# A fused linear-attention and mixture-of-experts kernel: the attention's scans read their second operand from PSUM, and the first tiles are issued in another order

## Chip, cores and metric

The kernel runs on one core of one Trainium2 chip. The metric is the device time of one execution in microseconds (us). Five engines work side by side, each through its own queue in order: PE (TensorE, matmuls), DVE (VectorE), ACT (ScalarE), POOL (GpSimd) and SP (SyncE, which here issues nearly all DMAs). They wait for one another through semaphores.

## The reference, cut to what matters

```
# gated linear attention, batch 4, 8 heads, 768 steps, head size 48
for t in range(768):
    state = alpha[t][:, None] * state + outer(k[t], v[t])
    y[t] = q[t] @ state
# y becomes x [3072, 384]; then a mixture of 8 experts, one expert per token:
xn, en = x / |x|, expert_emb / |expert_emb|
logits = xn @ en.T / tau
e = argmax(logits);  gate = softmax(logits)[e]
x2 = gate * (relu(x @ w1[e]) @ w2[e])
# then a dense layer pair with an ELU between
h = x2 @ w_in;  out = where(h > 0, h, exp(h) - 1) @ w_out
```

Everything is float32.

## The kernel before, in words

The program has three stages: attention with routing (the first 172 us of the profiled execution), the experts (to about 440 us) and the dense pair (to the end). The change touches only the first.

**Attention.** The 768 steps are cut into six chunks of 128, and with four batches there are 24 tiles, numbered 0 to 23, chunk by chunk. A tile holds eight heads as four pairs in the free dimension (`NP`), with 112 partitions for the two heads of a pair. For every tile the decays `alpha` are turned into running products. DVE does this with two scans over the 517 columns of the tile's `at` (four segments of 129 and one more column):

- `stR` (L332): the scan `R` (L340) runs backwards with multiply and then max against the tile `back`; it gives the product from a step to the chunk's end. A small reciprocal (L341) of each segment's first value goes into the tile `fore`. POOL then multiplies the keys: `Kh = k * R` (L343).
- `stA` (L345): the scan `A` (L350) runs forwards with multiply and then add of `fore`, so each segment starts from that reciprocal. POOL multiplies the queries: `Qh = q * A` (L352).

The two second operands, `back` and `fore`, are tiles of 112x517 in SBUF, as are `at`, `R` and `A`.

The other steps of a tile: `stE` (L354) copies checkpoints of `A` on ACT. `stS` (L371) makes the scores `psS` on PE from `Kh` and `Qh`; `stP` (L382) multiplies them by the triangle on DVE, from PSUM, in two halves `P`. `stT` (L360) transposes `Kh` on PE, and ACT copies it to `Kt` (L367). `stC` (L391) makes `psY` on PE from `P` and `v` (and from the state `G` in all but the first chunk), ACT copies it to `yT` (L407), and PE makes the state's update `psU`. `stD` (L439) makes `psX` on PE from `yT` and `rhsX`, which holds the normed expert embeddings beside an identity: `psX` has the token rows and, added up by a DVE reduce (L451), the logits. `psX` has two PSUM buffers.

**The order of the turns.** A hand-written loop (`fast`, L636) takes one turn per tile. Turn i issues, in this order: the loads of tile i+4 (for `v`, i+3), `stS` and `stT` of tile i+1, then `stR` of tile i+2, the first half of `stP` of tile i+1, `stA` of tile i+2, the second half of `stP`, the scatter of finished rows on POOL (`put`, L550), the reduces of the logits, pending routing work (`stR1`, `stR2`, small DVE operations on groups of two to six tiles), then `stD` of tile i-1, `stE` of tile i+2 and `stC` of tile i. Each engine follows this order within its own queue. So a tile's `Qh` is made one turn ahead of its `psS`.

**Before the loop** (L637 to L678): the first loads; 11 matmuls without use (`warm`, L281, L651) that keep PE active; `stR` and `stA` of tiles 0 and 1; the square sum of the embeddings on ACT (L668); `stS`, `stT` and `stP` of tile 0; casts of three constants on DVE. The embeddings' norm is a Newton iteration (`inv_norm1`, L127) in small DVE operations that stand in the queue `todo` and run in turns 0 and 1; the scaling of the embeddings (L675) and their transposition (`eT`, L725) close turn 1, and `stD` of tiles 0 and 1 both follow in turn 2.

Of the kernel before, what the change touches and what calls it, by code (L numbers as in the profile page):

```python
# [8 lines left out]
F32 = mybir.dt.float32  # L9
# [17 lines left out]
TP = T + 1  # L27
SW = H // 2 * TP + 1
# [20 lines left out]
A_FLOOR = 1e-15  # L49
# [12 lines left out]
def fused_kernel(ctx, tc, qk, a, v, emb, w12, wi, wo, cst, sel, cols, out):  # L62
# [64 lines left out]
    def inv_norm1(pool, x):  # L127

        shape = [x.shape[0], 1]
        y = pool.tile(shape, F32, name="rs_y1")  # L130
        t = pool.tile(shape, F32, name="rs_t1")
        h = pool.tile(shape, F32, name="rs_h1")
        yi = y.bitcast(I32)
        steps = [
            lambda: nc.vector.tensor_scalar(yi, x.bitcast(I32), 1, None, op0=ALU.logical_shift_right),
            lambda: nc.vector.tensor_scalar(h, x, -0.5, None, op0=ALU.mult),
            lambda: nc.vector.tensor_scalar(yi, yi, -1.0, float(0x5F3759DF), op0=ALU.mult, op1=ALU.add),
        ]
# [148 lines left out]
    def attention():  # L287
        with ExitStack() as st:
# [15 lines left out]
            back = gp.tile([C2, SW], F32, name="back")  # L304
            fore = [gp.tile([C2, SW], F32, name=f"fore{i}") for i in range(2)]
# [4 lines left out]

            def seg(t, n=TP):

                return t[:, :NP * TP].rearrange("c (p t) -> c p t", t=TP)

# [17 lines left out]
            def stR(i):  # L332

                if i >= NT:
                    return
                R = Rs[i] = wk.tile([C2, SW], F32, name="R")
                nc.vector.tensor_tensor_scan(R[:, ::-1], at[i][:, ::-1], back[:, ::-1], 0.0, op0=ALU.mult, op1=ALU.max)  # L340
                nc.vector.reciprocal(seg(fore[i % 2])[:, :, 0:1], seg(R)[:, :, 1:2])  # L341
                Kh[i] = wk.tile([C2, NP, T], F32, name="Kh")
                nc.gpsimd.tensor_tensor(Kh[i], qkt[i][:, 1], R[:, 1:].rearrange("c (p t) -> c p t", t=TP)[:, :, 1:], op=ALU.mult)  # L343

            def stA(i):  # L345

                if i >= NT:
                    return
                A = As[i] = wk.tile([C2, SW], F32, name="A")
                nc.vector.tensor_tensor_scan(A, at.pop(i), fore[i % 2], 0.0, op0=ALU.mult, op1=ALU.add)  # L350
                Qh[i] = wk.tile([C2, NP, T], F32, bufs=3, name="Qh")
                nc.gpsimd.tensor_tensor(Qh[i], qkt.pop(i)[:, 0], seg(A)[:, :, 1:], op=ALU.mult)  # L352

            def stE(i):  # L354
                if i < NT:
                    nc.scalar.activation(out=chk[:, i], in_=seg(As.pop(i))[:, :, 0:TP:T], func=AF.Copy)
# [68 lines left out]
            def stH(i):  # L425

                if i >= NT:
                    return
                r = Rs.pop(i)
                if i >= B:  # L430
                    g = G[i % B]
                    for p in range(NP):
                        nc.scalar.activation(out=g[:, p, :D], in_=g[:, p, :D], func=AF.Copy, scale=seg(r)[:, p, 1:2])
# [5 lines left out]
            def stD(i, keep=False):  # L439
# [4 lines left out]
                x = psD.tile([128, NP, 128], F32, name="psX")  # L444
# [73 lines left out]

            def stR2(g):
# [3 lines left out]
                r = ps1.tile([128, 8, E], F32, tag="psT" if g == NG - 2 else "psR", name="psR")[:, :n]  # L523
# [50 lines left out]
            def general():  # L574
# [15 lines left out]
                with tc.For_i(0, NC, 1) as cc, tc.For_i(0, T // TB, 1) as tb:  # L590
                    ts = bass.ds(tb * TB, TB)
                    for b in range(B):
                        for p in range(NP):
                            for h2 in range(2):
                                p0 = (b * H + 2 * p + h2) * EG
                                ch = slice(h2 * HP, h2 * HP + D)
                                for nm, src in (("a", a[bass.ds(cc, 1), ch, b, bass.ds(tb * TB + (p * TP + 1), TB)]),
                                                ("k", qk[bass.ds(cc, 1), ch, b, 1, p, ts]),
                                                ("q", qk[bass.ds(cc, 1), ch, b, 0, p, ts])):
                                    nc.sync.dma_start(out=rows[nm][p0:p0 + EG], in_=src.to_broadcast([EG, D, TB]))  # L600
# [35 lines left out]
            def fast():  # L636
# [14 lines left out]
                warm(ps1, "psY", 11)  # L651
                nc.scalar.activation(out=warm_t, in_=ones, func=AF.Exp)
                nc.vector.memset(back, A_FLOOR)
                nc.vector.memset(back[:, 1:].rearrange("c (p t) -> c p t", t=TP)[:, :, T:], 1.0)
                nc.vector.memset(cum[:, 0], 0.0)
                for t in fore + G:
                    nc.gpsimd.memset(t, 0.0)
                zero = xp.tile([128, 1, XW], F32, tag="xt", name="zero")
                nc.gpsimd.memset(zero, 0.0)
                for j in range(2):  # L660
                    stR(j)
                    stA(j)
                    stE(j)
                    stH(j)
                rows, rtau = emb_t[:, :2 * NP * HP], emb_t[:, 2 * NP * HP:]
                es = sm.tile([E, 1], F32, name="es")
                esq = wk.tile([E, 2 * NP * HP], BF16, bufs=1, tag="junk", name="esq")
                nc.scalar.activation(out=esq, in_=rows, func=AF.Square, accum_out=es)  # L668
                en, steps = inv_norm1(sm, es)
                stS(0)  # L670
                stT(0)
                stP(0, 0)
                stP(0, 1)
                todo.extend([lambda: nc.vector.reciprocal(rtau, rtau)] + steps
                            + [lambda: nc.vector.tensor_scalar(rows, rows, en, rtau, op0=ALU.mult, op1=ALU.mult)])  # L675
                nc.vector.tensor_tensor(strict16, c["tri"], c["ident"], op=ALU.subtract)
                nc.vector.tensor_copy(ident16, c["ident"])
                nc.vector.tensor_copy(base16[:, 0], c["base"])  # L678
# [3 lines left out]
                for i in range(tail):  # L682
# [9 lines left out]
                    if i - 3 in last:  # L692
                        todo[:0] = stR2(last[i - 3])
                    stR(i + 2)
                    stP(i + 1, 0)
                    stA(i + 2)
# [18 lines left out]
                    if i == 2:  # L715
                        stD(0)
                    if i > 1:
# [3 lines left out]
                    if i == 1:  # L721
                        step(len(todo))
                        eT = ps1.tile([128, NP, E], F32, tag="psR", name="eT")
                        for p in range(NP):
                            nc.tensor.transpose(eT[:, p], rows[:, p * 128:(p + 1) * 128], c["ident"][:E, :E])  # L725
                        nc.vector.tensor_copy(rhsX[:, :, CW:CW + E], eT)
# [21 lines left out]
            def decays():  # L748
# [3 lines left out]
                t = ps1.tile([1, 1], F32, tag="psR", name="psB")  # L752
# [14 lines left out]
            def ending():  # L767
# [9 lines left out]
                stP(i + 1, 1)  # L777
                r = stR2(g2 - 1)
# [446 lines left out]
def _layout(inputs):  # L1225
# [70 lines left out]
```

## Time and profile before

| what | us |
|---|---|
| three runs | 806.57, 808.1, 811.5 (median 808.1) |
| the profiled execution's own time | 807.42 |
| its span, from its first to its last instruction | 805.6 |
| attention with routing, up to the first expert matmul | 172.0 |
| mean granted TensorE clock, share of full speed | 0.988 |

The profile records one execution. Its span lies 1.8 us below its own time, and that time 0.7 us below the median of the runs. Times in rows are counted from the span's start. In a timeline row the columns are: start in us, length in us, engine, line, operation, output<-inputs, partitions x elements, and in brackets the engine's idle time before it and what ended that. A row with a count (x16) takes neighbouring instructions together.

### The profile page before, as it was taken

Reading aid. Unit: us, or ns where it says so; the run is one execution under the profiler, and the core shown is the slowest. Engines: PE = TensorE matmul, PEld = TensorE weight load, DVE = VectorE, ACT = ScalarE, POOL = GpSimd, SP = SyncE. Lnnn points to the kernel's source line nnn. Section 1 sums busy time; section 2 is a strip of 40 time slices with the busy share of each in tenths; the row PEclk is TensorE's granted clock in tenths of the full one; section 3 lists DMA queues with packets and bytes.
Section 4 is the critical chain, followed back from the end, with each engine's and each line's share of the span. In section 5 each row is a group of like instructions: output and inputs, shape, how many; then the busy total and the mean of one; then the engine's idle time right before and its main releaser. Section 6 shows DMA issues by size and latency. Waiting matters only on the chain.

```text
span 805.6 us, 13707 instructions
## 1 busy us (share of the span) xinstructions
PE 774.2 (96%) x5064; PEld 700.7 (87%) x5064; DVE 538.6 (67%) x1015; ACT 358.0 (44%) x783; POOL 190.1 (24%) x218
## 2 busy tenths in 40 slices
PE   7799998889999999999999999999999999999996
PEld 5688877669999999999988899999999999999996
DVE  7779999956877788888467665454545545545442
ACT  2466877624554555555355443333333333323331
POOL 6433656612333343343000020010002002002002
PEclk7899999999999999999999999999999999999999
DMA  9988863266656557563000010000001001000001
GB/s 246 255 237 216 229 182 95 109 196 157 194 184 206 179 193 231 173 213 111 1 0 1 2 40 1 0 11 31 1 1 39 1 1 40 0 1 30 11 1 39
DMA packets 44805, 77.72 MB, mean 96 GB/s; under 512 B 11958, under 2 KB 18230, under 8 KB 44734
## 3 DMA queue, kind: packets, MB, share of 16 engines
q1 hardware_dynamic: 41662, 67.36, 28.9%
q0 software_dynamic: 3072, 9.45, 3.2%
q8 instruction: 40, 0.66, 0.4%
q14 instruction: 31, 0.25, 0.1%
HBM read 64.58 MB, written 12.22 MB: 95 GB/s over the span
## 4 chain that ended last, share of the span: by engine, by line
PE 39%; issue 30%; DVE 3%; POOL 2%; ACT 2%; POOLq 0%; ACTq 0%
PE h L1144 6%; PE y L988 5%; PE y L990 4%; PE y L989 4%; PE h L957 4%; PE h L958 4%; PE h L956 4%; POOL out_dram L1178 2%; PE o L1167 2%; PE o L1165 2%; PE o L1166 2%; PE t L937 1%; DVE dlo L260 1%; DVE g L1150 1%; DVE mn L1146 1%
## 5 line engine op out<-in xcount | busy, mean ns | idle before, releaser
L1146 DVE TENSOR_SCALAR mn<-h 128x512 f32<-128x512 f32 x96 | 66.2, 690 | 139.7 <-PE h L1144 139.7
L1147 ACT ACTIVATE mn<-mn 128x512 f32<-128x512 f32 x96 | 60.7, 633 | 171.9 <-DVE mn L1146 171.9
L1167 PE MATMUL o<-dwo,gl 128*128 128x384 f32 x384 | 129.4, 337 | 1.4 <-DVE gl L1154 1.4
L1166 PE MATMUL o<-dlo,gh 128*128 128x384 f32 x384 | 128.4, 334 | 0.0
L1165 PE MATMUL o<-dwo,gh 128*128 128x384 f32 x384 | 128.2, 334 | 0.0
L1144 PE MATMUL h<-xh,dwi 128*128 128x512 f32 x288 | 112.8, 391 | 0.6 <-ACT x2T L1002 0.6
L1144 PE MATMUL h<-xh,dlo 128*128 128x512 f32 x288 | 113.2, 393 | 0.0
L1144 PE MATMUL h<-xl,dwi 128*128 128x512 f32 x288 | 112.5, 392 | 0.0
L1178 POOL DMA_INDIRECT out_dram<-ob,ids x24 | 23.2, 966 | 341.8 <-ACT ob L1175 338.1
L1153 ACT ACTIVATE gh<-g 128x512 fp32r<-128x512 f32 x96 | 60.7, 633 | 77.6 <-DVE g L1150 77.6
L960 ACT ACTIVATE hh<-h 128x432 fp32r<-128x432 f32 (+6 forms) x64 | 32.4, 507 | 106.2 <-PE h L958 99.1
L204 DVE TENSOR_TENSOR wlo<-raw,whi 128x512 fp32r<-128x512 f32 x96 | 73.2, 789 | 5.6 <-ACT whi L201 4.8
L1150 DVE SCALAR_TENSOR_TENSOR g<-mn,h 128x512 f32<-128x512 f32 x96 | 66.1, 688 | 15.2 <-ACT mn L1147 14.7
L1165 PEld LDWEIGHTS o<-dwo,gh 128*128 128x128 f32 x384 | 72.0, 187 | 4.2
L1166 PEld LDWEIGHTS o<-dlo,gh 128*128 128x128 f32 x384 | 72.0, 187 | 4.0
L1167 PEld LDWEIGHTS o<-dwo,gl 128*128 128x128 f32 x384 | 72.2, 188 | 2.1 <-DVE gl L1154 1.7
L961 DVE SCALAR_TENSOR_TENSOR hl<-h,hh 128x432 fp32r<-128x432 f32 (+6 forms) x64 | 36.7, 573 | 47.6 <-ACT hh L960 46.2
L988 PE MATMUL y<-hh,whi 128*128 128x432 f32 (+6 forms) x192 | 68.4, 356 | 0.0
L956 PE MATMUL h<-xh,whi 128*128 128x432 f32 (+6 forms) x192 | 66.5, 346 | 0.7 <-ACTq L1015 0.7
L244 POOL TENSOR_SCALAR dg<-dg 128x384 f32<-128x384 f32 x32 | 42.0, 1312 | 106.3 <-ACT dg L243 106.2
L1154 DVE TENSOR_TENSOR gl<-g,gh 128x512 fp32r<-128x512 f32 x96 | 65.7, 684 | 1.2 <-ACT gh L1153 1.1
L958 PE MATMUL h<-xh,wlo 128*128 128x432 f32 (+6 forms) x192 | 66.4, 346 | 0.0
(210 smaller groups left out, 1520.5 us busy)
## 6 DMA issues: line engine op xcount, KB each, us to landing
raw<-in_w_dram SPq DMA_DIRECT2D x96, 256.0 KB, 3.3
qk<-in_qk_dram SPq DMA_DIRECT2D x40, 192.0 KB, 3.9
vt<-in_v_dram SPq DMA_DIRECT2D x24, 256.0 KB, 4.7
raw<-in_wi_dram SPq DMA_DIRECT2D x16, 384.0 KB, 4.3
raw<-in_wo_dram SPq DMA_DIRECT2D x16, 384.0 KB, 4.1
xr<-xs SPq DMA_DIRECT2D x7, 576.0 KB, 4.9
at<-in_alpha_dram SPq DMA_DIRECT2D x40, 96.9 KB, 3.0
xs<-zero SPq DMA_DIRECT2D x7, 288.8 KB, 5.5
```

What stands on the lines that cost most here:

```text
L204: nc.vector.tensor_tensor(l[:, sl], r, h[:, sl].bitcast(F32), op=ALU.subtract)
L956: nc.tensor.matmul(ps, wh, xh[:, kk], start=(kk == 0), stop=False)
L958: nc.tensor.matmul(ps, wl, xh[:, kk], start=False, stop=(kk == KD - 1))
L988: nc.tensor.matmul(acc[e][d], wh, hh, start=(f == 0), stop=False)
L1144: nc.tensor.matmul(ps, l, x, start=(n == 0), stop=(n == len(terms) - 1))
L1146: nc.vector.tensor_scalar(mn, ps, 0.0, None, op0=ALU.min)
L1147: nc.scalar.activation(out=mn, in_=mn, func=AF.Exp)
L1150: nc.vector.scalar_tensor_tensor(g, mn, -1.0, ps, op0=ALU.add, op1=ALU.max)
L1154: low.append(lambda: nc.vector.tensor_tensor(gl, g, gh.bitcast(F32), op=ALU.subtract))
L1165: nc.tensor.matmul(o_, gh[:, sl], wh, start=(f == 0), stop=False)
L1166: nc.tensor.matmul(o_, gh[:, sl], wl, start=False, stop=False)
L1167: nc.tensor.matmul(o_, gl[:, sl], wh, start=False, stop=(f == M - 1))
```

## The change

The scans take their second operand from PSUM. A new tile `pz` takes one PSUM bank; one column of it, set to 2^-50, is broadcast over the tile's width as `floor`. For that, `at` gets three more columns per segment (`LEAD`): a zero, a 1/floor and a place for the reciprocal, and a 1/floor at its end, so that a segment now has 132 columns and a tile 528. The scan `R` takes the max with `floor`; the scan `A` takes the max with it too, starts afresh at every segment through the zero and the 1/floor, and finds the reciprocal in `at` itself. The tiles `back` and `fore` are gone, with their memsets on DVE and POOL.

In the first tiles: the embeddings are loaded ahead of tile 1 instead of behind it; 20 matmuls without use stand at the start instead of 11, and 4 more behind `stT` of tile 0; the Newton iteration runs on ACT ahead of the loop (only its first guess stays on DVE), its last reciprocal and the scaling in turn 0, `eT` at the end of turn 0; `stD` of tile 0 comes in turn 1 and so on, one per turn. The casts of the constants go to turn 3, on ACT and POOL.

Since the bank of `psR` is now that of `pz`, the routing's count tile takes a buffer of `psX` in most groups (`count_tile`), and the pending reduces are issued ahead of it.

```diff
+LEAD = 3
+TP = LEAD + T + 1
+SW = NP * TP
+A_FLOOR = 2.0 ** -50
...
-        yi = y.bitcast(I32)
...
+        yi, vec, act = y.bitcast(I32), nc.vector, nc.scalar
+        first = [
+            lambda: vec.tensor_scalar(yi, x.bitcast(I32), 1, None, op0=ALU.logical_shift_right),
+            lambda: vec.tensor_scalar(yi, yi, -1.0, float(0x5F3759DF), op0=ALU.mult, op1=ALU.add),
+        ]
+        steps = [lambda: act.activation(out=h, in_=x, func=AF.Copy, scale=-0.5)]
         for _ in range(3):
             steps += [
+                lambda: act.activation(out=t, in_=y, func=AF.Copy, scale=h),
+                lambda: act.activation(out=t, in_=t, func=AF.Copy, scale=y),
+                lambda: act.activation(out=t, in_=t, func=AF.Copy, bias=1.5),
+                lambda: act.activation(out=y, in_=t, func=AF.Copy, scale=y),
             ]
+        steps += [lambda: act.activation(out=y, in_=y, func=AF.Copy, scale=x, bias=1e-6)]
...
-            back = gp.tile([C2, SW], F32, name="back")
-            fore = [gp.tile([C2, SW], F32, name=f"fore{i}") for i in range(2)]
+            pz = pz_p.tile([128, 512], F32, name="pz")
+            floor = pz[:C2, 0:1].to_broadcast([C2, SW])
...
-                nc.vector.tensor_tensor_scan(R[:, ::-1], at[i][:, ::-1], back[:, ::-1], 0.0, op0=ALU.mult, op1=ALU.max)
-                nc.vector.reciprocal(seg(fore[i % 2])[:, :, 0:1], seg(R)[:, :, 1:2])
+                nc.vector.tensor_tensor_scan(R[:, ::-1], at[i][:, ::-1], floor, A_FLOOR, op0=ALU.mult, op1=ALU.max)
+                nc.vector.reciprocal(seg(at[i])[:, :, LEAD - 1:LEAD], seg(R)[:, :, LEAD:LEAD + 1])
...
-                nc.vector.tensor_tensor_scan(A, at.pop(i), fore[i % 2], 0.0, op0=ALU.mult, op1=ALU.add)
+                nc.vector.tensor_tensor_scan(A, at.pop(i), floor, 0.0, op0=ALU.mult, op1=ALU.max)
...
+            def count_tile(g):
+
+                if pz is None:
+                    return ps1.tile([128, 8, E], F32, tag="psR", name="psR")
+                if g == NG - 1:
+                    return pz[:, 64:64 + 8 * E].rearrange("p (n e) -> p n e", e=E)
+                if g == NG - 2:
+                    return ps1.tile([128, 8, E], F32, tag="psT", name="psR")
+                return psD.tile([128, 8, E], F32, tag="psX", name="psR")
...
                 nc.sync.dma_start(out=cs, in_=cst)
+                nc.sync.dma_start(out=emb_t, in_=emb)
                 load(1)
                 load_v(0)
-                nc.sync.dma_start(out=emb_t, in_=emb)
...
-                warm(ps1, "psY", 11)
+                warm(ps1, "psY", 20)
...
                 stS(0)
                 stT(0)
+                warm(ps1, "psY", 4)
+                for f in guess:
+                    f()
+                nc.vector.reciprocal(rtau, rtau)
+                stE(1)
                 stP(0, 0)
                 stP(0, 1)
+                for f in newton:
+                    f()
...
                     stP(i + 1, 0)
+                    if i == 0:
+                        nc.vector.reciprocal(en, en)
+                        nc.scalar.activation(out=rows, in_=rows, func=AF.Copy, scale=en)
+                        nc.scalar.activation(out=rows, in_=rows, func=AF.Copy, scale=rtau)
                     stA(i + 2)
...
-                    if i == 2:
-                        stD(0)
-                    if i > 1:
+                    if i > 0:
                         stD(i - 1)
```

On DVE the instructions from the scan `A` of tile 1 to the scan `A` of tile 2 stand so before (`strict`, `ident` and `base` are the casts; the numbers behind `at` and `fore` are those of buffers):

```order
L350 SCALAR_TENSOR_TENSOR A<-at_123,fore_141 112x517
L387 TENSOR_TENSOR P<-psS,cs 128x512 x2
L676 TENSOR_TENSOR strict_69<-cs 128x128
L677 CAST ident_71<-cs 128x128
L678 CAST base_72<-cs 128x8
L340 SCALAR_TENSOR_TENSOR R<-at_124,back 112x517
L341 RECIPROCAL fore_140<-R 112x4
L387 TENSOR_TENSOR P<-psS,cs 128x512
L350 SCALAR_TENSOR_TENSOR A<-at_124,fore_140 112x517
```

And so in the changed kernel, with the Newton iteration's first guess in `rs_y`:

```order
L350 SCALAR_TENSOR_TENSOR A<-at_123,pz 112x528
L136 TENSOR_SCALAR rs_y_197<-es 8x1
L137 TENSOR_SCALAR rs_y_197<-rs_y_197 8x1
L685 RECIPROCAL emb_t<-emb_t 8x1
L387 TENSOR_TENSOR P<-psS,cs 128x512 x2
L340 SCALAR_TENSOR_TENSOR R<-at_124,pz 112x528
L341 RECIPROCAL at_124<-R 112x4
L387 TENSOR_TENSOR P<-psS,cs 128x512
L711 RECIPROCAL rs_y_197<-rs_y_197 8x1
L350 SCALAR_TENSOR_TENSOR A<-at_124,pz 112x528
```

The three casts have left, three tiny operations stand ahead of tile 0's `P`, and the reciprocal L711, which needs the end of the Newton iteration, now stands ahead of the scan `A` of tile 2.

On ACT, before, the queue runs so from the first `Kt` to the first `yT`:

```order
L367 ACTIVATE Kt<-psT 128x448 x2
L356 ACTIVATE chk<-A 112x8
L407 ACTIVATE yT<-psY 128x512
L423 ACTIVATE G_135<-psU 112x4x48
L367 ACTIVATE Kt<-psT 128x448
```

In the changed kernel the Newton iteration and the scaling stand between the `Kt` of tile 0 and that of tile 1, and between that and `yT`; these are the last six of the iteration's fourteen rows and what follows:

```order
L145 ACTIVATE rs_y_197<-rs_t_198,rs_y_197 8x1
L142 ACTIVATE rs_t_198<-rs_y_197,rs_h_199 8x1
L143 ACTIVATE rs_t_198<-rs_t_198,rs_y_197 8x1
L144 ACTIVATE rs_t_198<-rs_t_198 8x1
L145 ACTIVATE rs_y_197<-rs_t_198,rs_y_197 8x1
L147 ACTIVATE rs_y_197<-rs_y_197,es 8x1
L367 ACTIVATE Kt<-psT 128x448
L712 ACTIVATE emb_t<-emb_t,rs_y_197 8x512
L713 ACTIVATE emb_t<-emb_t 8x512
L356 ACTIVATE chk<-A 112x8
L407 ACTIVATE yT<-psY 128x512
L741 ACTIVATE rhsX<-eT 128x4x8
```

So ACT works through fourteen 8x1 operations before it copies tile 1's `Kt`, and the scaled embeddings follow at once.

On PE, before, the end of turn 1 and the start of turn 2 read so:

```order
L415 MATMUL psU<-vt_131,Kt 48x48
L725 MATMUL eT<-cs,emb_t 128x8 x4
L380 MATMUL psS<-Qh,Kh 128x128 x8
L364 MATMUL psT<-cs,Kh 128x112 x4
L446 MATMUL psX<-rhsX,yT 128x104 x8
L405 MATMUL psY<-P,vt_132 64x128 x8
```

And in the changed kernel the end of turn 0 and the start of turn 1:

```order
L415 MATMUL psU<-vt_130,Kt 48x48
L740 MATMUL eT<-cs,emb_t 128x8 x4
L380 MATMUL psS<-Qh,Kh 128x128 x8
L364 MATMUL psT<-cs,Kh 128x112 x4
L446 MATMUL psX<-rhsX,yT 128x104 x4
L405 MATMUL psY<-P,vt_131 64x128 x8
```

`eT` has moved up by a whole turn, and `psX` of tiles 0 and 1, which stood together, are now a turn apart.

## Rows read from the trace of the kernel before

**Rows 1.** Stretches: us; busy PE, PEld, DVE, ACT, POOL; PEclk, DMA share, GB/s.

```profile
40.00:60.00 20.00, 20.00 (x274) 17.21 (x276) 15.23 (x21) 12.77 (x42) 7.28 (x8) 1.00 0.85 236
...
60.00:135.00 75.00, 71.45 (x998) 60.09 (x996) 72.87 (x163) 54.17 (x172) 41.33 (x44) 1.00 0.70 193
```

**Rows 2.** Scans on DVE, grouped by line, 60.5 to 134.7 us: busy us, mean ns.

```profile
L350 DVE TENSOR_TENSOR_SCAN A<-at,fore 112x517 f32<-112x517 f32 x12 | 22.8, 1896 | 0.0
...
L340 DVE TENSOR_TENSOR_SCAN R<-at,back 112x517 f32<-112x517 f32 x12 | 14.7, 1228 | 0.0
```

**Rows 3.** Timeline of DVE and POOL around one multiply of POOL.

```profile
63.93 0.66 DVE L387 TENSOR_TENSOR P<-psS,cs 128x512 f32<-128x512 f32 x1
63.93 1.18 POOL L343 TENSOR_TENSOR Kh<-qk,R 112x512 f32<-112x512 f32 x1 [2.76 <-DVE R L340]
...
64.51 1.70 DVE L350 TENSOR_TENSOR_SCAN A<-at,fore 112x517 f32<-112x517 f32 x1
```

**Rows 4.** Timeline of DVE: a product of two SBUF operands, POOL idle.

```profile
157.14 0.67 DVE L204 TENSOR_TENSOR wlo<-raw,whi 128x512 fp32r<-128x512 f32 x1
```

**Rows 5.** Timeline of PE: one whole turn, and the last turns of the loop.

```profile
91.38 1.16 PE L380 MATMUL psS<-Qh,Kh 48*128 48x128 f32 x16
...
92.91 1.05 PE L446 MATMUL psX<-rhsX,yT 128*128 128x104 f32 x8
93.89 1.09 PE L402 MATMUL psY<-Qh,G 48*64 48x128 f32 x16
94.91 1.09 PE L405 MATMUL psY<-P,vt 128*64 128x128 f32 x16
95.93 0.58 PE L412 MATMUL psU<-G,cs 112*112 112x192 f32 x2
96.44 0.67 PE L415 MATMUL psU<-vt,Kt 128*64 128x48 f32 x16
97.04 1.16 PE L380 MATMUL psS<-Qh,Kh 48*128 48x128 f32 x16
...
134.80 1.16 PE L380 MATMUL psS<-Qh,Kh 48*128 48x128 f32 x16 [1.27 <-POOL tick L555]
...
146.01 1.11 PE L446 MATMUL psX<-rhsX,yT 128*128 128x104 f32 x8 [1.28 <-ACT yT L407]
147.05 1.16 PE L380 MATMUL psS<-Qh,Kh 48*128 48x128 f32 x16
```

**Rows 6.** Timeline of PE: the warmings, psS of tiles 0, 2, 3 and 6, and eT.

```profile
1.15 4.40 PE L285 MATMUL warm<-ones 128*128 128x512 bf16 x11 [1.15 <-DVE ones L650]
9.87 2.08 PE L380 MATMUL psS<-Qh,Kh 48*128 48x128 f32 x16 [4.32 <-POOL Qh L352]
...
18.70 1.16 PE L380 MATMUL psS<-Qh,Kh 48*128 48x128 f32 x16
...
25.12 0.41 PE L725 MATMUL eT<-cs,emb_t 8*128 8x8 f32 x4 [3.25 <-DVE emb_t L675]
25.46 2.08 PE L380 MATMUL psS<-Qh,Kh 48*128 48x128 f32 x16
...
45.49 1.16 PE L380 MATMUL psS<-Qh,Kh 48*128 48x128 f32 x16
```

**Rows 7.** A stretch of 2 us, with the columns of rows 1.

```profile
36.00:38.00 2.00, 0.68 (x6) 0.71 (x7) 2.00 (x5) 0.00 (x0) 1.18 (x1) 1.00 0.75 221
```

**Rows 8.** Timeline of POOL and ACT: first multiply, a checkpoint copy, embeddings' squares, scaling of G.

```profile
5.64 2.12 POOL L343 TENSOR_TENSOR Kh<-qk,R 112x512 f32<-112x512 f32 x1 [2.46 <-DVE fore L341]
...
6.82 0.21 ACT L356 ACTIVATE chk<-A 112x8 f32<-112x8 f32 x1 [4.50 <-DVE A L350]
...
11.06 0.61 ACT L668 ACTIVATE esq<-emb_t 8x512 bf16<-8x512 f32 x1
...
33.64 1.00 ACT L433 ACTIVATE G<-G,R 112x48 f32<-112x48 f32 x4
```

**Rows 9.** DMA traffic of the first 40 us.

```profile
DMA packets 5244, 10.04 MB, mean 251 GB/s; under 512 B 1222, under 2 KB 2182, under 8 KB 5241
```

More of the change, by code (lines that the diff above doesn't have):

```diff
@@ L443, in stD @@
                 y = yT.pop(i)
-                x = psD.tile([128, NP, 128], F32, name="psX")
+                x = psD.tile([128, NP, 128], F32, tag="psX", name="psX")
                 for p in range(NP):
@@ L522, in stR2 @@
                 s3 = [128, n, E]
-                r = ps1.tile([128, 8, E], F32, tag="psT" if g == NG - 2 else "psR", name="psR")[:, :n]
+                r = count_tile(g)[:, :n]
                 o_ = oh[:, i0:i0 + n]
@@ L650, in fast @@
                 nc.vector.memset(ones, 1.0)
-                warm(ps1, "psY", 11)
+                warm(ps1, "psY", 20)
                 nc.scalar.activation(out=warm_t, in_=ones, func=AF.Exp)
-                nc.vector.memset(back, A_FLOOR)
-                nc.vector.memset(back[:, 1:].rearrange("c (p t) -> c p t", t=TP)[:, :, T:], 1.0)
+                nc.vector.memset(pz[:, 0:1], A_FLOOR)
                 nc.vector.memset(cum[:, 0], 0.0)
-                for t in fore + G:
+                for t in G:
                     nc.gpsimd.memset(t, 0.0)
@@ L659, in fast @@
                 nc.gpsimd.memset(zero, 0.0)
+                rows, rtau = emb_t[:, :2 * NP * HP], emb_t[:, 2 * NP * HP:]
+                es = sm.tile([E, 1], F32, name="es")
+                esq = wk.tile([E, 2 * NP * HP], BF16, bufs=1, tag="junk", name="esq")
+                en, guess, newton = inv_norm1(sm, es)
                 for j in range(2):
@@ L662, in fast @@
                     stA(j)
-                    stE(j)
                     stH(j)
[L665 to L669, printed above, removed]
+                    if j == 0:
+                        stE(j)
+                        nc.scalar.activation(out=esq, in_=rows, func=AF.Square, accum_out=es)
                 stS(0)
                 stT(0)
+                warm(ps1, "psY", 4)
[3 more added lines that the diff above has]
+                stE(1)
                 stP(0, 0)
                 stP(0, 1)
[L674 to L678, printed above, removed]
+                for f in newton:
+                    f()
                 lag = []
@@ L692, in fast @@
                     if i - 3 in last:
+                        while late:
+                            late.pop(0)()
                         todo[:0] = stR2(last[i - 3])
@@ L751, in decays @@
                 g2 = sm.tile([C2, 1], F32, name="g2")
-                t = ps1.tile([1, 1], F32, tag="psR", name="psB")
+                t = pz[:1, 256:257]
                 d = chk[:, :, :, 1:2].rearrange("p n a o -> p (n a) o")
@@ L777, in ending @@
                 stP(i + 1, 1)
+                late.pop(0)()
                 r = stR2(g2 - 1)
```

51 lines of the change are left out of this document (22 added, 29 removed).

## The prediction

> **What bounds the kernel now.** The sum is made against the profiled execution: its span of 805.6 us and 1.8 us around it. I read the busy time by stretches first. From 40 to 60 us PE is busy without a break; from 60 to 135 us it is busy 71.45 of 75 us and DVE 72.87 [rows 1]. So PE bounds the attention's turns from 40 us on, and DVE is so full that PE waits for it in some. PE's own turn is 97.04 - 91.38 = 5.66 us, with no idle time in it [rows 5].
>
> DVE's load is partly not its own. By the groups of its lines the scan `R` takes 1.23 us and the scan `A` of the same width 1.90 on average [rows 2]. The timeline says why: POOL's multiply `Kh` runs from 63.93 to 65.11, and the `A` that starts under it at 64.51 takes 1.70, that is 0.47 more than a scan alone. The product `P`, wholly under the same `Kh`, takes 0.66, and `Kh` its 1.18 [rows 3]. `P` reads one operand from PSUM, `A` reads both from SBUF. When DVE is first, POOL pays: the first `Kh`, under a scan, takes 2.12 us [rows 8]. So a DVE operation with two SBUF operands and a POOL multiply hold each other up, and one with an operand in PSUM does not.
>
> Last the first tiles, in PE's timeline. The `psS` of tiles 0, 2, 3 and 6 start at 9.87, 18.70, 25.46 and 45.49 [rows 6]; the last three turns take 20 us, more than a full turn each. [...] In 36 to 38 us PE was busy 0.68 of 2 us and the granted clock stayed at 1.00 [rows 7].
>
> **The change, part by part.**
>
> *The scan itself.* No row shows a scan with a PSUM operand. 528 columns for 517 are 0.03 us on 1.23. A product of 512 columns takes 0.66 with one operand in PSUM [rows 3] and 0.67 with both in SBUF while POOL rests [rows 4], so at the low end the operand's place gains 0.01; the high end is the 1.90 that `A` takes now [rows 2]. I take 1.26, from the row of `P`, the nearest in kind. [...]
>
> *DVE in the later turns.* In 60 to 135 us twelve `A` lose 1.90 - 1.26 = 0.64 each, 7.7 us, and twelve `R` gain 0.03 each. DVE falls from 72.87 to some 65.5 us, 5.0 per turn against PE's 5.66. So PE ends last, and what is gained is PE's waiting alone: 75 - 71.45 = 3.55 us [rows 1]. Two turns behind that have no `psT` and no `psU`. PE needs there 5.66 less 1.11 (`psU`, 95.93 to 97.04) and 0.4 (`psT`, between the end of `psS` and 92.91), 4.15; they took 147.05 - 134.80 = 12.25 us [rows 5]. In one of them `psX` waited 1.28 for `yT`, which stands behind the checkpoint of a held-up `A` in ACT's queue. With short scans the chain psS, `P`, `A`, `Qh` (1.16 + 0.66 + 1.26 + 1.18 and gaps, 4.4) or DVE with a group's last three operations (4.7) ends last in the first; the second goes through `psY`, `yT` and `psX`, some 5.9. So 10.6 for 12.25. Together 3.5 + 1.6 = 5.1; I take 5.
>
> *The first tiles*, by start times. Tile 0's scans end at 6.85 as before, since its load ends last there. `Kh` takes 1.18 for 2.12, `Qh` follows `A` at 6.95, and `psS` 0 starts at 8.2 for 9.87. `R` and `A` of tile 1 run unhindered to 9.6, `Qh` to 10.9: `psS` 1 at 10.95. DVE then does three tiny operations (0.45), both `P` (1.3) and `R` of tile 2 to 12.6, one `P` to 13.4, and comes to the reciprocal L711, which waits for ACT. There, behind `Kt` of tile 0 and the checkpoint (10.65), stand 14 dependent operations. Four have constants, like the checkpoint copy with 0.21; ten take a scale per partition, like the scaling of G, whose four rows run in 1.00 us, 0.25 from start to start and some 0.3 each [rows 8]. Bounds are 14 x 0.20 = 2.8 and 14 x 0.35 = 4.9; I take 4 x 0.23 + 10 x 0.31 = 4.0, by the kind of each. So L711 runs at 14.65, a new wait of 1.3 us on DVE with `A` of tile 2 and all later scans behind it, and through `Qh` POOL and PE. `A` ends at 16.1, `Qh` at 17.4: `psS` 2 at 17.45 for 18.70. Meanwhile ACT copies `Kt` of tile 1 (0.55) and scales the embeddings twice (0.61 [rows 8] and 0.1 for the scale, each): `eT` at 16.6, ahead of `psS` 2 and hidden. From there the clock decides. [...]
>
> *The warmings.* 11 took 4.40 us, 0.40 each [rows 6]. 20 at that pace end at 9.2; if the clock rises behind ten of them, at 7.2. `psS` 0 comes at 8.2, so this costs it nothing or 1 us; I take nothing. The four more fill PE's time between `psT` 0 and `psS` 1. PE then idles from about 14.2 (`psS` 1 at 10.95, and 1.1 + 0.4 + 1.0 + 0.6 behind it) to 16.6. The clock fell behind 3.25 us of idle time and stayed through the stretch of rows 7; which of them this gap is like I can't tell. If it falls, I reckon with six us at half speed, as long as the low level lasted before: 3 us less, `psS` 6 at 39.5. Between 9 and 6 I take 8.
>
> *What costs nothing.* The embeddings' load delays tile 1's by one issue, and `R` 1 waits for `A` 0 anyway. The reduces ahead of the count tile run when their `psX` is long done. The casts in turn 3 lie beside idle time of ACT and POOL. 11 columns more are 2% of one load.
>
> *The sum*: 8 + 5 = 13 us off the attention. The experts and the dense pair are PE's own work and only start earlier. 807.42 - 13 = 794.4 for an execution like the profiled one, which is 0.7 below the median of the runs shown; from that median it is 795.1. I predict 795.0.
>
> **The rivals.**
>
> *The first tiles give most back.* The Newton chain takes 4.9, the clock falls and stays low until `psX` of tile 1: 3 us gained there and 5 later, 807.4 - 8 = 799.5. For it: a gap of 2.4 us, and DVE's queue behind ACT. Against: far more matmuls stand ahead of the gap than did.
>
> *The loads end last.* 10.04 MB came in the first 40 us at 251 GB/s, nearly without pause [rows 9]. Up to tile 7's `at` and `qk` 8.2 MB are needed (eight tiles of 0.70, six `v` of 0.26, constants and one fill), at that rate by 33 us, and `R` 7 is due at about 34. If the rate falls to the 236 of the next stretch [rows 1], the turns slip by 2 us: 797.
>
> *The scan is still held up.* If POOL blocks a scan with one PSUM operand as one with two from SBUF, the later turns keep their waits and the first tiles gain about 4: 803.5. The row of `P` speaks against it. [...]
>
> *Slower: a PSUM scan is dear.* DVE has 5.66 - 5.0 = 0.66 us to spare per turn, 0.33 per scan, so from 1.6 us per scan DVE bounds the turns, and from about 1.8 the loss eats the first tiles' gain. At 1.9 DVE needs 6.3 per turn, 0.6 more than the 5.7 now; over 17 turns that loses 10 us against 6 gained before: 811. For it: no such row exists, and a scan depends on its last result as a product does not. Against: the products' rows.
>
> **How the numbers follow.** The forecast (clock up or down in the gap) 0.66; first tiles give back 0.14; loads 0.09; still held up 0.07; dear scan 0.04. A measurement of this kernel tells about 1% (8 us) from no change. Faster by over 1%, below 800.0: 0.66 + 0.09 + half of 0.14 = 0.82; within 1%: 0.14; slower 0.04. The forecast's own range is 791.5 (full clock, and later turns a little better) to 798; with the second and third case it reaches 801. I give 790.5 to 801.
>
> **What would show it.** Right: every `R` and `A` at 1.25 to 1.3 us, also under a multiply of POOL; POOL's multiplies at 1.18 from the first on; PE busy nearly without break from tile 6 to tile 20; `psS` 2 near 17.5 and `psS` 6 between 36 and 40; L711 waiting for ACT a little over 1 us. Wrong: scans above 1.5 us; `psS` rows of 2.08 us later than the gap; scans that wait for `at`; or an attention that ends earlier while the experts wait for weights.

## The result and the profile after the change

The changed kernel takes 795.77 us (median of 4 runs, 795.04 to 796.08) against 807.38 (4 runs, 806.57 to 811.5) of the kernel before: a ratio of 0.983, 95% interval 0.9806 to 0.9853. The profiled execution took 795.64 us, with a span of 793.9.

| start of, us | before | after | gained up to here |
|---|---|---|---|
| `psS` of tile 6 | 45.49 | 37.76 | 7.73 |
| `psS` of tile 23, the last | 147.05 | 133.93 | 13.12 |
| first expert matmul | 171.95 | 160.29 | 11.66 |
| end of the span | 805.6 | 793.9 | 11.7 |

So the first tiles gave 7.7 us, the later turns 5.4, and the end of the attention gave 1.5 back; from there on nothing changed. Line numbers below are those of the kernel that is shown.

Stretches after the change, in the columns of [rows 1]; the second holds fourteen turns, from `psS` 6 to `psS` 20, and the last two are a place in the attention's end:

```profile
60.00:135.00 75.00, 73.85 (x1021) 62.74 (x1020) 70.27 (x164) 59.32 (x190) 47.75 (x53) 1.00 0.74 196
37.76:118.04 80.28, 80.10 (x1117) 68.03 (x1115) 71.70 (x165) 58.15 (x185) 44.93 (x45) 1.00 0.90 239
138.00:140.00 2.00, 2.00 (x22) 1.67 (x22) 1.83 (x7) 0.45 (x1) 0.16 (x2) 0.55 0.26 99
140.00:142.00 2.00, 2.00 (x24) 1.67 (x22) 1.91 (x18) 1.33 (x5) 0.08 (x1) 0.60 0.03 8
```

And the same fourteen turns before the change:

```profile
45.49:128.15 82.66, 80.39 (x1116) 68.01 (x1115) 77.24 (x160) 58.67 (x186) 43.66 (x44) 1.00 0.77 212
```

In these turns PE's idle time falls from 2.27 us to 0.18: almost nothing holds it up any more. DVE's busy time falls from 77.24 to 71.70 us, that is to 5.1 per turn. From 60 to 135 us DVE is still busy 70.27 us for 72.87, since more turns fall into that stretch.

The groups by line, 60.5 to 134.7 us, as in [rows 2], with POOL's multiplies:

```profile
L352 POOL TENSOR_TENSOR Qh<-qk,A 112x512 f32<-112x512 f32 x13 | 16.6, 1280 | 9.2 <-DVE A L350 9.2
L343 POOL TENSOR_TENSOR Kh<-qk,R 112x512 f32<-112x512 f32 x13 | 16.5, 1272 | 15.7 <-DVE R L340 6.8 <-PE psS L380 4.3 <-PE psR L539 2.2
L340 DVE TENSOR_TENSOR_SCAN R<-at,pz 112x528 f32<-112x528 f32 x13 | 16.2, 1247 | 0.0
L350 DVE TENSOR_TENSOR_SCAN A<-at,pz 112x528 f32<-112x528 f32 x13 | 16.2, 1243 | 0.0
```

Both scans take 1.24 to 1.25 us, with or without a multiply beside them. The multiplies take 1.27 to 1.28, not the 1.18 of before.

PE's first tiles, to be laid beside [rows 6]:

```profile
1.15 6.41 PE L284 MATMUL warm<-ones 128*128 128x512 bf16 x20 [1.15 <-DVE pz L663]
8.43 1.16 PE L380 MATMUL psS<-Qh,Kh 48*128 48x128 f32 x16 [0.87 <-POOL Qh L352]
...
11.48 1.16 PE L380 MATMUL psS<-Qh,Kh 48*128 48x128 f32 x16 [0.49 <-POOL Qh L352]
...
16.70 0.41 PE L740 MATMUL eT<-cs,emb_t 8*128 8x8 f32 x4 [2.05 <-ACT emb_t L713]
17.63 1.16 PE L380 MATMUL psS<-Qh,Kh 48*128 48x128 f32 x16 [0.52 <-POOL Qh L352]
18.72 1.01 PE L364 MATMUL psT<-cs,Kh 112*128 112x112 f32 x4
19.52 1.90 PE L446 MATMUL psX<-rhsX,yT 128*128 128x104 f32 x8
...
23.19 1.16 PE L380 MATMUL psS<-Qh,Kh 48*128 48x128 f32 x16
...
37.76 1.16 PE L380 MATMUL psS<-Qh,Kh 48*128 48x128 f32 x16
```

`psS` 0 and 1 now take 1.16 us each, at a granted clock of 1.00 from 8 to 14 us. PE idles 2.05 us ahead of `eT`, and behind `psS` 2 the clock is at its low level (0.50 granted from 20 to 22 us): `psT` takes 1.01 us and `psX` 1.90, for 0.60 and 1.05 in later turns.

DVE in the same stretch, and the Newton iteration's kinds of operations on ACT (by line, 10 to 16.5 us):

```profile
7.31 1.25 DVE L340 TENSOR_TENSOR_SCAN R<-at,pz 112x528 f32<-112x528 f32 x1 [0.74 <-DMA at<-in_alpha_dram]
...
14.89 0.15 DVE L711 RECIPROCAL rs_y<-rs_y 8x1 f32<-8x1 f32 x1 [1.41 <-ACT rs_y L147]
14.97 1.25 DVE L350 TENSOR_TENSOR_SCAN A<-at,pz 112x528 f32<-112x528 f32 x1
```

```profile
L142 ACT ACTIVATE rs_t<-rs_y,rs_h 8x1 f32<-8x1 f32 x3 | 0.9, 294 | 0.1
...
L144 ACT ACTIVATE rs_t<-rs_t 8x1 f32<-8x1 f32 x3 | 0.6, 202 | 0.1
```

The end of the attention, on PE and DVE, first before and then after the change:

```profile
148.14 0.19 PE L525 MATMUL psR<-base,ident 128*128 128x32 bf16 x1
...
148.38 1.09 PE L402 MATMUL psY<-Qh,G 48*64 48x128 f32 x16
...
171.95 0.46 PE L956 MATMUL h<-xh,whi 128*128 128x432 f32 x1
```

```profile
133.93 1.16 PE L380 MATMUL psS<-Qh,Kh 48*128 48x128 f32 x16
135.12 1.29 DVE L387 TENSOR_TENSOR P<-psS,cs 128x512 f32<-128x512 f32 x2 [0.92 <-PE psS L380]
136.33 0.18 DVE L451 TENSOR_REDUCE lg<-psX 128x8 f32<-128x32 f32 x1
136.57 0.19 PE L535 MATMUL psR<-base,ident 128*128 128x32 bf16 x1 [1.47 <-DVE lg L451]
...
136.81 1.09 PE L402 MATMUL psY<-Qh,G 48*64 48x128 f32 x16
137.83 1.68 PE L405 MATMUL psY<-P,vt 128*64 128x128 f32 x16
139.44 1.97 PE L402 MATMUL psY<-Qh,G 48*64 48x128 f32 x16
...
160.29 0.46 PE L977 MATMUL h<-xh,whi 128*128 128x432 f32 x1
```

Before, the count tile `psR` had a bank of its own and followed `psS` 23 at once. Now it takes a buffer of `psX`, so it waits for the reduce that reads that buffer, and the reduce stands behind both `P` of tile 23. PE idles 1.47 us, and from 138 to 142 us the granted clock is 0.55 and 0.60.

### The profile page after: what moved, and what is told of

Same layout as the page of the kernel before. It is cut to its first block, busy times and chain, and to the rows that moved or that the text cites. A ratio compares the mean times of both kernels' runs of the same rounds, so it can differ in the third digit from the quotient of the medians.

```text
span 793.9 us, 13732 instructions
## 1 busy us (share of the span) xinstructions
PE 772.5 (97%) x5077; PEld 698.2 (88%) x5077; DVE 523.3 (66%) x1001; ACT 362.7 (46%) x802; POOL 189.4 (24%) x217
## 4 chain that ended last, share of the span: by engine, by line
PE 40%; issue 30%; DVE 3%; POOL 3%; ACT 2%; POOLq 0%; ACTq 0%
PE h L1165 6%; PE y L1009 5%; PE y L1011 4%; PE y L1010 4%; PE h L978 4%; PE h L979 4%; PE h L977 4%; POOL out_dram L1199 2%; PE o L1188 2%; PE o L1186 2%; PE o L1187 2%; PE t L958 1%; DVE dlo L259 1%; DVE g L1171 1%; DVE mn L1167 1%
## 5 line engine op out<-in xcount | busy, mean ns | idle before, releaser
L981 ACT ACTIVATE hh<-h 128x432 fp32r<-128x432 f32 (+6 forms) x64 | 32.4, 507 | 105.4 <-PE h L979 98.3
L978 PE MATMUL h<-xl,whi 128*128 128x432 f32 (+6 forms) x192 | 66.2, 345 | 0.2 <-DVEq L1036 0.2
```

The lines of the kernel that those rows point to most:

```text
L978: nc.tensor.matmul(ps, wh, xl[:, kk], start=False, stop=False)
```

## The experiments

The theory was the prediction's: the scans were held up by POOL's multiplies through their second SBUF operand; the first tiles gain by their new order besides. The rivals: the gain has another cause (the single broadcast column, or the new order alone); each added wait costs nothing. The kernel before was timed beside each of three sets of runs, each set on another chip, with medians of 809.99, 809.88 and 811.89 us. So times are compared as ratios to it, and what is under 2 us is read from start times.

### The place of the second operand

```diff
-            floor = pz[:C2, 0:1].to_broadcast([C2, SW])
+            fl = gp.tile([C2, 1], F32, name="fl")
+            floor = fl.to_broadcast([C2, SW])
...
-                nc.vector.memset(pz[:, 0:1], A_FLOOR)
+                nc.vector.memset(fl, A_FLOOR)
```

> The changed kernel with one edit: the column that the scans broadcast lies in SBUF again, all else stays (528 columns, the new first tiles). Theory, the operand's place: scans under a multiply of POOL are held up again; in the later turns A takes about 1.9 us on average and R about 1.23, the first Kh about 2.1 for 1.28, psS 6 starts 2 to 4 us later than 37.76, the later turns lose about 5 us again: 801 to 805 us. Rival, the single broadcast column (or the other form of the recurrence) is what is cheap, not PSUM: scans stay at 1.25 us and the time at 795 to 796.

Measured: 808.01 us, ratio 0.9986 (0.9967 to 1.0006): no gain is left, where 801 to 805 us were expected. The scans by line, 60.5 to 134.7 us:

```profile
L351 DVE TENSOR_TENSOR_SCAN A<-at,fl 112x528 f32<-112x528 f32 x13 | 27.2, 2091 | 0.0
...
L341 DVE TENSOR_TENSOR_SCAN R<-at,fl 112x528 f32<-112x528 f32 x12 | 15.0, 1250 | 0.0
```

And `psS` of tiles 6 and 23 on PE:

```profile
39.64 1.16 PE L381 MATMUL psS<-Qh,Kh 48*128 48x128 f32 x16
...
145.05 1.16 PE L381 MATMUL psS<-Qh,Kh 48*128 48x128 f32 x16
```

The column is broadcast as before; only its memory differs, and `A` is held up again. So the place of the operand is shown to be the cause. But the sum is worse than the theory had it: the later turns take 145.05 - 39.64 = 105.4 us, 3.9 more than in the kernel before (101.6). The stretch of the rows above holds other turns in each kernel. Over the same fourteen turns, `psS` 6 to `psS` 20, `A` takes 1.90 us on average for 1.77 in the kernel before, `R` 1.39 for 1.32 (so it is held up too), the multiplies 1.28 for 1.18, and DVE is busy 81.48 us for 77.24. That the longer multiplies are the reason was not tried.

### The new order of the first tiles alone left out

```diff
-                warm(ps1, "psY", 20)
+                warm(ps1, "psY", 11)
...
-                    if i > 0:
+                    if i == 2:
+                        stD(0)
+                    if i > 1:
                         stD(i - 1)
```

With it the embeddings' load, the iteration on DVE, `eT` in turn 1 and the casts stand as before, and the four later matmuls without use are gone.

> The changed scans, but the first tiles in the order of the kernel before: 11 matmuls without use, embeddings loaded behind tile 1 and normed on DVE, eT in turn 1, the first two psX in turn 2, casts on DVE ahead of the loop. Theory, two parts that add up: the later turns (from psS 6 to psS 23) take 96 us as in the changed kernel, for 101.6 before; psS 6 starts at 41 to 43 (before 45.49, changed 37.76), since the scans alone give the first tiles 3 to 4 us; 799 to 801 us. Rival, the new order is worth all of the first tiles' gain: psS 6 at 45, 803 us. Second rival, the scans alone are worth it: psS 6 at 38, 796 us.

Measured: 802.6 us, ratio 0.9913 (0.9888 to 0.9938). The time lies above the 799 to 801 expected; the ratio, taken of the 807.38 us of the result, is 800.4. PE's first tiles, and `psS` 6 and 23:

```profile
11.47 2.08 PE L382 MATMUL psS<-Qh,Kh 48*128 48x128 f32 x16 [1.59 <-POOL Qh L354]
...
23.05 0.41 PE L738 MATMUL eT<-cs,emb_t 8*128 8x8 f32 x4 [3.00 <-DVE emb_t L686]
23.39 2.08 PE L382 MATMUL psS<-Qh,Kh 48*128 48x128 f32 x16
...
43.45 1.16 PE L382 MATMUL psS<-Qh,Kh 48*128 48x128 f32 x16
...
139.62 1.16 PE L382 MATMUL psS<-Qh,Kh 48*128 48x128 f32 x16
```

`psS` 6 starts at 43.45 and `psS` 23 at 139.62: 96.17 us, to the hundredth what the changed kernel takes (133.93 - 37.76). Up to `psS` 6 the scans alone gain 2.04 us, the new order alone (the experiment before) 5.85, together 7.73. These are two parts that add up, to 0.2 us; the scans' share in the first tiles was overestimated (2 for 3 to 4), since PE still waits 3.00 us for `eT` and the clock falls (0.83 granted on average from 20 to 40 us; `psS` 3 takes 2.08 us).

### The warmings

```diff
-                warm(ps1, "psY", 20)
+                warm(ps1, "psY", 11)
...
-                warm(ps1, "psY", 4)
```

> The changed kernel with 11 matmuls without use at the start instead of 20, and without the four behind psT of tile 0. Theory, the more of them hold the clock: PE idles some 3 us ahead of psS 0, psS 1 or what follows it runs at the low level (2.08 us for 16 rows), and since the wait for the Newton iteration hides part of that, psS 6 starts 1 to 2.5 us later than 37.76: 797 to 798.5 us. Rival, the wait for the iteration and the clock's fall behind it hide all of it: psS 6 at 37.8, 795.8 us.

Measured: 796.99 us, ratio 0.9837; the time alone does not tell it from the changed kernel. The starts do:

```profile
8.16 2.08 PE L380 MATMUL psS<-Qh,Kh 48*128 48x128 f32 x16 [2.86 <-POOL Qh L352]
...
18.67 2.08 PE L380 MATMUL psS<-Qh,Kh 48*128 48x128 f32 x16 [0.33 <-POOL Qh L352]
...
40.14 1.16 PE L380 MATMUL psS<-Qh,Kh 48*128 48x128 f32 x16
```

PE idles 2.86 us ahead of `psS` 0 and runs at the low level up to the matmuls ahead of `psS` 3 (`psS` 0, 1 and 2 take 2.08 us each, 0.50 granted from 16 to 24 us). `psS` 6 comes 2.4 us later: the theory's upper end.

### The gap ahead of eT

```diff
                     if i == 0:
+                        warm(psD, "psX", 8)
                         eT = psD.tile([128, NP, E], F32, tag="psX", name="eT")
```

> The changed kernel with eight matmuls without use between psU of tile 0 and eT, where PE idled 2.05 us and the clock fell behind it. Theory, the fall cost 1.3 us: psS 2 as before at 17.6, psT, psX and psY behind it at full clock (0.60, 1.05 and 1.09 us), psS 3 at 22.0 for 23.19, psS 6 at 36.5 for 37.76: 794.5 us. Rival, the clock falls all the same, or the chain through Qh sets psS 3: 23.2 and 37.8, 795.8 us.

Measured: 794.6 us, ratio 0.981 (0.9794 to 0.9825).

```profile
14.57 1.90 PE L284 MATMUL warm<-ones 128*128 128x512 bf16 x8
...
18.84 1.05 PE L446 MATMUL psX<-rhsX,yT 128*128 128x104 f32 x8
...
21.76 1.16 PE L380 MATMUL psS<-Qh,Kh 48*128 48x128 f32 x16 [0.40 <-POOL Qh L352]
```

`psX` takes 1.05 us for 1.90, `psS` 3 starts 1.43 us earlier and `psS` 6, at 36.34, 1.42. Of that, 0.32 us lie ahead of `psS` 2 already (17.31 for 17.63): tile 0's `qk` was there that much earlier in this execution (its `Kh` starts at 5.57 for 5.89). From `psS` 2 to `psS` 3 it is 4.45 us for 5.56. So the fall of the clock cost 1.1 us, and no more: it ended before `psS` 3.

### The wait for the Newton iteration

```diff
+                    stA(i + 2)
                     if i == 0:
                         nc.vector.reciprocal(en, en)
...
-                    stA(i + 2)
```

`eT` and the copy to `rhsX` move to turn 1, ahead of `stD(0)`.

> The changed kernel with the reciprocal that waits for the Newton iteration, and the scaling, issued behind the scan A of tile 2, and eT in turn 1 ahead of the first psX. Theory, that wait of 1.41 us on DVE stands on the first tiles' path: A of tile 2 starts at 13.5 for 14.97, psS 2 at 16.2 for 17.63, psS 3 to 6 each 1.4 us earlier or more (psS 6 at 36.3 for 37.76): 794.3 us. Rival, the gap in PE's work or the embeddings' scaling holds the first psX up anyway: psS 3 and psS 6 no earlier than 23.2 and 37.8, 795.8 us.

Measured: 795.14 us, ratio 0.9829; its five runs spread from 792.95 to 797.07.

```profile
15.91 1.16 PE L380 MATMUL psS<-Qh,Kh 48*128 48x128 f32 x16 [1.28 <-POOL Qh L352]
...
35.44 1.16 PE L380 MATMUL psS<-Qh,Kh 48*128 48x128 f32 x16
```

`psS` 2 starts 1.72 us earlier and `psS` 6 2.32: the wait stood on the path. The granted clock is 1.00 in all of the first 40 us here; the gap ahead of `psS` 2 is 1.28 us. So the 2.32 hold what the clock's fall had cost as well: against the kernel with the gap filled, where the clock held too (1.00 in the first 40 us, `psS` 6 at 36.34), the edit gains 0.90. The profile is of the run of 792.95 us, with a mean granted clock of 0.998; the other four have 0.991 to 0.995, so the clock fell in them somewhere.

### The count tile

```diff
+                if g == NG - 3:
+                    return pz[:, 128:128 + 8 * E].rearrange("p (n e) -> p n e", e=E)
                 return psD.tile([128, 8, E], F32, tag="psX", name="psR")
...
                 stP(i + 1, 1)
-                late.pop(0)()
                 r = stR2(g2 - 1)
```

> The changed kernel with the count tile of the third group from the end in free columns of the bank pz instead of a buffer of psX, and without the reduce that was issued ahead of it. Theory, that wait took back what the turns gained: psR there runs without idle time ahead of it right behind psS 23, psY of tile 22 starts at 135.3 for 136.81, the granted clock stays at 1.00 from 134 to 142, the first expert matmul comes at 158.8 for 160.29: 1.4 us less than the changed kernel, 794.4. Rival, something else ends last between the last psS and the first expert matmul (the routing's chain on DVE, the rows' gather): that matmul stays at 160.3 and the time at 795.8.

Measured: 794.95 us, ratio 0.9823 (0.98 to 0.9845).

```profile
134.92 0.19 PE L537 MATMUL pz<-base,ident 128*128 128x32 bf16 x1
...
135.17 1.09 PE L402 MATMUL psY<-Qh,G 48*64 48x128 f32 x16
136.19 1.09 PE L405 MATMUL psY<-P,vt 128*64 128x128 f32 x16
```

The wait is gone, the granted clock stays at 1.00 from 134 to 160 us, and the first expert matmul comes at 158.40 for 160.29. The cleaner mark is the first matmul ahead of it that gathers rows by a one-hot tile (`t<-hot,xt`). From `psS` 23 to this one-hot matmul it took 15.47 us in the kernel before (147.05 to 162.52), 16.62 in the changed kernel (133.93 to 150.55), and takes 15.48 here (133.83 to 149.31). So 1.15 of the 1.46 us that the result's table shows as lost stand here, and the edit gives 1.14 of them back. The rest lies behind the one-hot matmul, where PE waits for transfers and the profiles differ by some tenths (9.43 us before, 9.74 changed, 9.09 here).

The kernel of the section above tells the two parts of the 1.15 apart. It has the same wait ahead of the count tile, but the clock held behind it (1.00 granted from 134 to 160 us):

```profile
134.26 0.19 PE L535 MATMUL psR<-base,ident 128*128 128x32 bf16 x1 [1.48 <-DVE lg L451]
...
134.50 1.09 PE L402 MATMUL psY<-Qh,G 48*64 48x128 f32 x16
```

There it is 15.94 us from `psS` 23 to the one-hot matmul (131.62 to 147.56). So, by one profile each, the wait costs some 0.5 us and the clock's fall some 0.7.

### POOL's multiplies

```diff
-LEAD = 3
+LEAD = 4
...
-    steps[..., :LEAD] = 0.0, 1.0 / A_FLOOR, 1.0
+    steps[..., :LEAD] = 0.0, 0.0, 1.0 / A_FLOOR, 1.0
```

> The changed kernel with one more column per segment (133 for 132), the same scans otherwise. In the changed kernel every multiply of POOL takes 1.28 us for 1.18 before, and so with the column in SBUF too, so it is not the scan's PSUM operand. Theory, it is the place or stride of the columns that POOL reads (129 apart before, 132 now): at 133 the multiplies take 1.18 again, and the first tiles' chain, which has one Qh per tile, is 0.1 us shorter per tile. Rival, something else in the change: 1.28 stays. The time moves by less than 1 us in both.

Measured: 795.21 us (2 runs), ratio 0.9817. The multiplies by line, 60.5 to 134.7 us:

```profile
L343 POOL TENSOR_TENSOR Kh<-qk,R 112x512 f32<-112x512 f32 x13 | 15.5, 1190 | 15.8 <-DVE R L340 6.8 <-PE psS L380 4.2 <-PE psR L539 2.2
L352 POOL TENSOR_TENSOR Qh<-qk,A 112x512 f32<-112x512 f32 x13 | 15.4, 1184 | 11.1 <-DVE A L350 9.5 <-DMA qk<-in_qk_dram 1.6
```

With 133 columns per segment they take 1.19 us again, with 132 it was 1.28. So the layout cost 0.09 us each; which property of it (the distance of the rows, their first column) was not tried. From `psS` 3 on each of the first chunk's turns takes 4.37 us for 4.46. `psS` 6 starts at 36.47 for 37.76, most of it because the clock held in this profile (1.00 granted in the first 40 us): from `psS` 2 to `psS` 3 it is 4.37 us for 5.56.

### The embeddings' load

```diff
-                nc.sync.dma_start(out=emb_t, in_=emb)
                 load(1)
+                nc.sync.dma_start(out=emb_t, in_=emb)
                 load_v(0)
```

> The changed kernel with the embeddings' load behind tile 1's two loads instead of ahead of them. Theory, R of tile 1 no longer waits for its load (0.74 us), psS 1 comes 0.4 to 0.6 us earlier, but psS 2 stays at 17.6, since the Newton iteration on ACT, which starts from the embeddings' squares and the Kt of tile 0, holds the scan A of tile 2: no gain from psS 2 on. Rival, all of the first tiles move up with R: psS 2 at 17.1 and psS 6 at 37.3.

Measured: 797.33 us, one execution. `R` of tile 1 still waits 0.49 us for its load, and POOL's multiply behind it 1.13 us for `qk`; `psS` 1 starts at 11.77, not earlier. From `psS` 2 on (17.48) nothing is gained. So tile 1 waits for its data in either order; in the changed kernel on the same chip (below) `R` of tile 1 waits 0.47 us. When its load is there differs between executions by more than the order makes: over the profiles that have the new order and the scans' operand in PSUM, `R` of tile 1 starts between 6.83 and 7.64 us, here at 6.95.

### Together, and the changed kernel again

The count tile and the iteration's edit in one kernel:

> Both edits that gained at their place: the count tile in free columns of pz, and the reciprocal with the scaling behind the scan A of tile 2 with eT a turn later. Theory, they lie in different stretches and add up: psS 6 at 35.4, the first matmul on the gathered rows' one-hot at 146.3 for 150.55, span 789.5 to 790.5 us, time 791.5 to 792.5 (in executions whose clock falls nowhere else). Rival, behind psS 23 the routing's chain on DVE ends last and takes the second part back: 147.5, 793 us.

Measured: 792.54 us (5 runs, 792.31 to 795.69), ratio 0.9795 (0.9776 to 0.9814). `psS` 6 starts at 35.42, the one-hot matmul at 147.08, and the span is 790.5 us. The two add up: against the changed kernel the one-hot matmul is 3.47 us earlier, and `psS` 23 alone 2.32 (131.61); the count tile alone had given 1.24 there. The 146.3 expected was 0.8 too low: it took the one-hot matmul of the iteration's profile, 147.56, less 1.24, but in that profile the clock had held at the attention's end, so that the fall's 0.7 us were counted twice.

These two, the 133 columns, the later load, and the scaling behind the second `P`; beside it the changed kernel, on the same chip:

> The changed kernel with what gained or cost something in the runs before: the count tile in free columns of pz, the reciprocal with the scaling behind the scan A of tile 2 and the product behind it, eT a turn later, 133 columns per segment, and the embeddings' load behind tile 1's. Theory, the gains add up, since each has its own place on the path: psS 1 at 10.9 for 11.48, psS 2 at 15.2 for 17.63, psS 6 at 34.4 for 37.76, psS 23 at 130.4 for 133.93, and the time 791 to 792 us against 795 to 796 of the changed kernel on the same chip. Rival, the loads end last once the turns run ahead of them (scans waiting for at, multiplies for qk): psS 6 no earlier than 35.4, 792.5 us or more.

> The changed kernel once more, on the same chip and beside the same runs of the kernel before as the combined edits. Theory: 795 to 796 us, the gap of 2 us ahead of eT and a fall of the clock behind it, psS 3 at 23.1. Rival, the fall comes in some executions alone: psS 3 at 22 and 794.5 us in this profile.

Measured: 792.64 us (5 runs, 792.51 to 794.05), ratio 0.9777 (0.9753 to 0.9801), against 798.47 us (5 runs, 797.83 to 801.06), ratio 0.9844 (0.982 to 0.9867), of the changed kernel. The combined edits beat both kernels, the changed one by 5.8 us here. Both expectations of the time were missed, 791 to 792 us and 795 to 796; the kernel before is slower on this chip too (811.89).

The last three edits add next to nothing to the first two: `psS` 6 starts at 35.39, where 34.4 was expected and 35.42 stood without them. The rival, that the loads end last, is what this shows:

```profile
7.34 1.26 DVE L340 TENSOR_TENSOR_SCAN R<-at,pz 112x532 f32<-112x532 f32 x1 [0.62 <-DMA at<-in_alpha_dram]
```

`R` of tile 1 waits 0.62 us for its `at`. From there DVE works on without a pause to `A` of tile 2, and `Qh` of tile 2 waits 0.68 us for that scan. `Kh` of tile 1 also waits 0.90 us for `qk`, and that of tile 2 1.47. But tile 0's own load came 0.29 us later in this profile than in that of the two edits (its `R` starts at 3.94 for 3.65), so some 0.3 us of gain can be hidden; one profile each does not tell.

In the second profile of the changed kernel, of its run of 801.06 us, the clock fell again in the gap ahead of `eT` (2.17 us), and `psS` 3 came at 24.11, 6.79 us behind `psS` 2 (0.50 granted from 18 to 22 us): the fall cost 2.3 us here. It fell in the count tile's profile as well, which has the same first tiles (a gap of 2.09 us, 0.50 granted from 20 to 22 us). The rival, a fall in some executions alone, is not excluded: with 133 columns the gap was 1.75 us and the clock held, with the later load it was 1.62 and the clock fell.

## Why the prediction was right, and where not

The time forecast was 795.0 us and 795.77 was measured, by the mechanism that the prediction named. Its 13 us off the attention were 11.7. That the time came closer than the gain is chance: the forecast stood on a median of 808.1 us for the kernel before, where four runs gave 807.38. Term by term:

- **The scan itself: right.** 1.26 us forecast from the row of `P`, 1.245 measured, also under a multiply. The nearest row in kind told it: 1.245 us for 528 columns with an operand in PSUM against 1.228 for 517 with both in SBUF [rows 2], and the 11 columns are, as an estimate from 1.228 x 11 / 517, 0.03.
- **Who holds up whom: right.** The prediction read it from `P` and `A` under one `Kh` [rows 3], and the kernel with the column in SBUF shows it for a scan with all else equal (`A` at 1.24 us with the column in PSUM, 2.09 with it in SBUF).
- **The later turns: right.** 5 us forecast, 13.12 - 7.73 = 5.39 measured. Of these the last two turns were to take 10.6 us for 12.25, and took 133.93 - 123.34 = 10.59. In the others PE was to lose its 3.55 us of waits, and they became 3.73 shorter. DVE was to need 5.0 us per turn and needed 5.1.
- **The first tiles: right, but for the price of the clock's fall.** The 9 us if the clock held and the 6 if it fell, between which the 8 was taken, were the author's estimates, and no run shows the 8 as such; the runs showed 9.15 us with the gap filled, where the clock held (`psS` 6 at 36.34), and 7.73 in the result, where it fell. The iteration (4.0 forecast, 4.1 measured), the wait of L711 (1.3 and 1.41) and `eT` (16.6 and 16.70) came as worked out. The clock fell, as left open; that cost 1.1 us in the result's profile and 2.3 in the second one, not the 3 reckoned from how long the low level had lasted before. That the 8 met the 7.73 measured is in part luck.
- **"`R` 1 waits for `A` 0 anyway": wrong.** Tile 1's load ended last: 0.74 us of waiting on DVE, and `psS` 1 at 11.48 for 10.95. Of this 0.22 come from `A` 0, which ended at 6.57 for 6.79: the cover that hid the transfer was itself shortened by the change. The rest is the load, there at 7.31 and before the change by 6.87 at the latest; as it moves that much between executions, what the embeddings' load ahead of it adds is not shown. It cost nothing only because the iteration held tile 2 longer.
- **POOL's multiplies at 1.18: wrong, by 0.1 us.** The 132 columns made it 1.28. The price was taken from a row of the old layout.
- **"The reduces ahead of the count tile run when their `psX` is long done": wrong in the last group but two.** True of the reduce's input; but the reduce stands behind two `P` that wait for `psS` 23. It cost 1.15 of the 1.46 us that the attention's end gave back, without which the sum would nearly have been met (12.8 for 13); the count tile in its own columns gave 1.14 back. The prediction had priced this edit at nothing without following DVE's queue at that place.
- **The rival "still held up" was underpriced.** 803.5 us was forecast for it; made real, with the column in SBUF, it gives no gain at all. It had the later turns as before, but in that kernel they are 3.9 us longer; why is open.

## What to carry to other kernels

Where an operation takes longer beside another engine's, as `A` did here beside POOL's multiplies (2.09 us on average with both operands in SBUF, 1.24 with one in PSUM), look for a row in which one operand of the busy engine already lies elsewhere; it prices the move before it is made, and one small constant operand may be enough to move. When a buffer or a bank is taken away from one user, follow the queue of the engine that frees the new one at every place of use, above all where the loop ends and the order differs. And when a stage gets faster, ask again of each transfer in it what hid it.

## What was not expected of the hardware

- POOL's multiply of 112x512 took 1.28 us with its scanned operand's segments 132 columns apart, and 1.19 with 133 (1.18 with 129 before). Between the first two kernels only that one column per segment differs.
- With both inputs in SBUF the scans `A` and `R` took 1.90 and 1.39 us on average beside multiplies of 1.28, and 1.77 and 1.32 beside multiplies of 1.18, over the same fourteen turns: a slightly longer neighbour went with a longer delay. That it is the cause was not tried.
- The clock's fall is not told by one gap alone: PE idled 1.75 us ahead of `eT` in one kernel and the granted clock held at 1.00, 1.62 in another and it fell to 0.50. In the second PE had also waited 1.02 and 1.08 us ahead of `psS` 0 and 1, in the first 0.23 and 0.80.
